# A new order of the work, and new engines for some of it, in an mLSTM and ELU feed-forward kernel

## The chip, the cores and the metric

The kernel runs on one core of a Trainium2 chip. The metric is the time of one execution on the device in microseconds (us). The core has five engines that run side by side: TensorE (PE in the rows; PEld is its loading of weights), VectorE (DVE), ScalarE (ACT), GpSimd (POOL) and SyncE (SP), which issues the transfers here. They wait for one another by semaphores. Transfers of data go over queue q1. Queue q8 moves instructions.

## What is computed

A recurrent attention (an mLSTM) over 768 steps, for 4 batches of 8 heads of size 40, and then a feed-forward layer with ELU on the 3072 rows of 320 that it gives:

```python
for t in range(S):
    m_new  = np.maximum(f_gate[:, :, t] + m, i_gate[:, :, t])
    f_stab = np.exp(f_gate[:, :, t] + m - m_new)
    i_stab = np.exp(i_gate[:, :, t] - m_new)
    C = f_stab * C + i_stab * np.einsum('bhd,bhe->bhde', vt, kt)
    n = f_stab * n + i_stab * kt
    h_tilde = np.einsum('bhde,bhe->bhd', C, qt)
    denom = np.maximum(np.abs(nq), 1.0)          # nq = n . qt
    y[:, :, t] = sigmoid(o_gate) * h_tilde / denom
h = x @ w_in                                     # 3072x320 by 320x2048
g = np.where(h > 0.0, h, np.exp(np.minimum(h, 0.0)) - 1.0)
out = g @ w_out                                  # 2048x320
```

## The kernel before

The 768 steps are cut into 6 chunks of 128. A chunk of a batch is a **tile**: 24 tiles, tile n being chunk n // 4 of batch n % 4. For each tile the kernel does the following.

- It loads q and k (line 671, into one of three buffers qk_148 to qk_150), v with k once more (677) and the output gate (682) as `vko`, and from chunk 1 on the decays `bb` (705) and `w` (695). Buffers are few, so a load waits until the last reader of its buffer is done.
- **Products** (752): 16 small matmuls of k with q for all heads. VectorE multiplies them with the decays (813).
- **Visit** (`outputs`): 32 matmuls of the state C with `bb` (833), 64 of the decayed products with v (841), and for all chunks but the last 32 of k with v for the new state (851). PE runs through all these in 1.7 us or so. VectorE or GpSimd shrinks C (868) and VectorE adds to it (879).
- **Output of the tile** (`xf`, `den`): ScalarE takes the absolute value of the denominator (886), VectorE bounds and inverts it (890, 891) and gates the output (899), VectorE or GpSimd multiplies (903), a small copy follows (342), and PE turns the result (917).

The feed-forward layer takes tiles in blocks of two or three (256 or 384 columns). For each of 16 slices of 128 of the hidden size there is a first layer of 8 matmuls (970), since each operand is split into a high and a low part, and an ELU: ScalarE (978, 981), VectorE (983), the high part `gh` by ScalarE (986), the low part `gl` by VectorE or GpSimd (988). The second layer has three matmuls for each tile (997): gh, gh, gl. Sums go to DRAM (1024) where a block is done in two goes. The weights are split on the chip as well, by conversions of many elementwise steps (lines 437 to 477), early in the kernel.

What sets the order: every operation is an `Op` with the engines that can do it and their costs. `Plan.run` is a greedy scheduler, which puts at each moment the ready operation of lowest **rank** on its engine. The rank follows from the tile or slice an operation belongs to, unless the table `PLACES` holds a number for its place (p13 for the products of tile 13 and what follows them, v13 for its visit, y13 for the output, qk13, vk13, o13, w13, bb13 for loads, c and d for conversions). The table `USES` names an engine for single operations ("p13.1" is the second operation at place p13; f is the feed-forward layer):

```python
    def at(self, place, rank):
        self.place = place
        self.rank = self.places.get(place, rank)
...
        use = self.uses.get(f"{self.place}.{nth}")
        if use is not None:
            o.engines = {use: engines[use]}
...
                    (o for o in pending if when[o] <= t), key=lambda o: (o.rank, -o.tail, o.number)
```

Where the plan leaves PE idle before 70 us, filler matmuls of ones (526) are put in. The code that comes out has no loops: each of the matmuls is an instruction of its own in the program.

Of the kernel before, what the change touches and what calls it, by code (L numbers as in the profile page):

```python
# [206 lines left out]
def tile_mlstm_then_elu_ffn(  # L207
# [48 lines left out]
    PLACES = {"clear": 7.1154181, "g0": -0.805181392, "qk0": -0.351178529, "v0":  # L256
# [22 lines left out]
    USES = {"clear.2": "POOL", "rows.0": "DVE", "rows.1": "DVE", "rows.2": "DVE",  # L279
        "states.0": "ACT", "states.2": "ACT", "g0.0": "ACT", "g0.7": "DVE", "p0.4": "ACT",  # L280
        "p0.8": "DVE", "y0.6": "DVE", "y0.8": "DVE", "p1.4": "ACT", "p1.10": "POOL", "v1.1":
        "ACT", "y1.6": "ACT", "p2.10": "POOL", "v2.1": "ACT", "p3.4": "ACT", "v3.1": "ACT",
# [4 lines left out]
        "ACT", "g2.2": "DVE", "g2.4": "POOL", "g2.10": "DVE", "p8.3": "ACT", "p8.9": "ACT",  # L287
# [19 lines left out]
        "ACT", "d3.0": "ACT", "d3.1": "DVE", "c4.0": "ACT", "c5.2": "POOL", "c6.1": "ACT",  # L307
# [5 lines left out]
        "ACT", "c17.0": "ACT", "c17.5": "DVE", "d17.0": "DVE", "f.5": "DVE", "f.12": "DVE",  # L313
# [821 lines left out]
```

## Time and profile before

| | |
|---|---|
| time, median of 3 runs | 470.45 us (469.73 to 471.0) |
| the profiled execution | 468.6 us |
| its span | 466.8 us |
| around the span | 1.8 us |
| PE busy | 98% |
| DVE, ACT, POOL busy | 72%, 60%, 22% |

The span goes from the first instruction to the last. A wait of an engine is idle time ahead of one of its instructions. The profile puts it down to the engine whose semaphore came last; where it finds none, it writes "issue".

### The profile page before, as it was taken

Reading aid. Unit: us, or ns where it says so; the run is one execution under the profiler, and the core shown is the slowest. Engines: PE = TensorE matmul, PEld = TensorE weight load, DVE = VectorE, ACT = ScalarE, POOL = GpSimd, SP = SyncE. Lnnn points to the kernel's source line nnn. Section 1 sums busy time; section 2 is a strip of 40 time slices with the busy share of each in tenths; the row PEclk is TensorE's granted clock in tenths of the full one; section 3 lists DMA queues with packets and bytes.
Section 4 is the critical chain, followed back from the end, with each engine's and each line's share of the span. In section 5 each row is a group of like instructions: output and inputs, shape, how many; then the busy total and the mean of one; then the engine's idle time right before and its main releaser. Section 6 shows DMA issues by size and latency. Waiting matters only on the chain.

```text
span 466.8 us, 13897 instructions
## 1 busy us (share of the span) xinstructions
PE 458.5 (98%) x5737; PEld 429.1 (92%) x5737; DVE 336.5 (72%) x698; ACT 277.9 (60%) x672; POOL 100.6 (22%) x137
## 2 busy tenths in 40 slices
PE   9899999999999999999999999999999999999996
PEld 4557799999999999989999999999999999999996
DVE  7899899899888878778887853587894754354432
ACT  5778678788866456454654565354545455545664
POOL 1226302320212031234111340131041201010011
PEclk9999999999999999999999999999999999999999
DMA  7956374334208361246405501353411301000100
GB/s 210 317 183 198 102 276 146 114 98 148 86 8 236 103 226 41 79 131 199 144 17 150 173 1 43 114 165 119 133 45 38 95 0 44 1 3 0 44 1 28
DMA packets 42175, 49.71 MB, mean 106 GB/s; under 512 B 3360, under 2 KB 34816, under 8 KB 42112
## 3 DMA queue, kind: packets, MB, share of 16 engines
q1 hardware_dynamic: 42112, 48.82, 33.6%
q8 instruction: 45, 0.74, 0.6%
q14 instruction: 18, 0.15, 0.1%
HBM read 43.42 MB, written 5.39 MB: 105 GB/s over the span
## 4 chain that ended last, share of the span: by engine, by line
PE 96%; DVE 2%; ACT 1%; issue 1%; DVEq 0%; ACTq 0%
PE h L970 39%; PE acc L997 36%; PE ps_a L752 6%; PE ps_a L841 3%; PE ps_a L833 3%; PE acc L526 3%; PE ps_a L917 2%; PE ps_a L851 1%; PE h L779 1%; PE h L485 1%; PE h L789 1%; PE h L783 1%; DVE gl L988 0%; DVE w L477 0%; DVE w L813 0%
## 5 line engine op out<-in xcount | busy, mean ns | idle before, releaser
L970 PE MATMUL h<-xh,w 128*128 128x384 f32 (+1 forms) x720 | 176.6, 321 | 0.0
L997 PE MATMUL acc<-w,gh 128*128 128x320 f32 x768 | 172.2, 311 | 0.9 <-ACT den L886 0.7
L997 PEld LDWEIGHTS acc<-w,gh 128*128 128x128 f32 x768 | 128.9, 188 | 2.6 <-issue 0.6
L983 DVE SCALAR_TENSOR_TENSOR e<-e,h 128x384 f32<-128x384 f32 (+1 forms) x144 | 72.7, 505 | 80.6 <-ACT e L981 79.9
L970 PEld LDWEIGHTS h<-xh,w 128*128 128x128 f32 x720 | 124.6, 188 | 1.7
L978 ACT ACTIVATE e<-h 128x384 f32<-128x384 f32 (+1 forms) x144 | 65.4, 454 | 93.3 <-PE h L970 85.4
L997 PE MATMUL acc<-w,gl 128*128 128x320 f32 x384 | 118.7, 309 | 0.5 <-DVE gl L988 0.5
L970 PE MATMUL h<-xl,w 128*128 128x384 f32 (+1 forms) x432 | 111.4, 317 | 0.0
L986 ACT CAST gh<-e 128x384 fp32r<-128x384 f32 (+1 forms) x144 | 68.1, 474 | 39.6 <-DVE e L983 38.5
L970 PEld LDWEIGHTS h<-xl,w 128*128 128x128 f32 x432 | 76.3, 188 | 0.0
L988 DVE TENSOR_TENSOR gl<-e,gh 128x384 fp32r<-128x384 f32 (+1 forms) x109 | 60.6, 558 | 20.0 <-ACT gh L986 19.7
L997 PEld LDWEIGHTS acc<-w,gl 128*128 128x128 f32 x384 | 72.0, 188 | 0.9 <-DVE gl L988 0.9
L981 ACT ACTIVATE e<-e 128x384 f32<-128x384 f32 (+1 forms) x144 | 70.5, 490 | 3.6
L988 POOL TENSOR_TENSOR gl<-e,gh 128x384 fp32r<-128x384 f32 (+1 forms) x35 | 33.5, 956 | 171.2 <-ACT gh L986 125.7
L796 DVE TENSOR_TENSOR_SCAN w<-w,ident 128x512 f32<-128x512 f32 x32 | 39.4, 1241 | 1.5 <-DMA w<-f_d 1.5
L813 DVE TENSOR_TENSOR w<-ps_a,w 128x512 f32<-128x512 f32 x48 | 31.4, 683 | 2.0 <-ACT wl L342 1.0
L752 PE MATMUL ps_a<-qk 40*128 40x128 f32 x384 | 29.9, 291 | 0.3 <-DVE xl L342 0.2
L752 PEld LDWEIGHTS ps_a<-qk 40*128 40x128 f32 x384 | 25.1, 193 | 5.2 <-issue 1.8
L903 POOL TENSOR_TENSOR xf<-xf,den 128x320 f32<-128x320 f32 x13 | 10.8, 831 | 45.0 <-DVE den L891 44.6
L841 PE MATMUL ps_a<-vko,w 128*32 128x41 f32 x1536 | 19.4, 201 | 1.0 <-DVE w L813 0.9
L841 PEld LDWEIGHTS ps_a<-vko,w 128*32 128x32 f32 x1536 | 17.7, 109 | 2.2 <-DVE w L813 1.5
L868 POOL TENSOR_TENSOR C<-C,dec 40x164 f32<-40x164 f32 x20 | 10.0, 498 | 33.2 <-PE ps_a L833 27.2
(114 smaller groups left out, 432.2 us busy)
## 6 DMA issues: line engine op xcount, KB each, us to landing
w<-f_d SPq DMA_DIRECT2D x32, 256.0 KB
vko<-in_vko SPq DMA_DIRECT2D x24, 324.0 KB
qk<-in_qk SPq DMA_DIRECT2D x48, 160.0 KB
wide<-in_w_out SPq DMA_DIRECT2D x8, 640.0 KB
wide<-in_w_in SPq DMA_DIRECT2D x8, 512.0 KB
vko<-in_vko SPq DMA_DIRECT2D x24, 160.0 KB
out<-os SPq DMA_DIRECT2D x24, 160.0 KB
bb<-b_d SPq DMA_DIRECT2D x40, 80.0 KB
```

The source lines that it names most:

```text
L526: nc.tensor.matmul(spare, ones, ones.unsqueeze(1).to_broadcast([P, 4, P]), start=True, stop=True, skip_group_check=True,)
L752: nc.tensor.matmul(ps(two, P, HH, L)[:, j, :], kt[rows, j, :], qt[rows, j, :], start=True, stop=True,)
L796: nc.vector.tensor_tensor_scan(a, a, ident4.rearrange("p h t -> p (h t)"), 0.0, op0=ALU.mult, op1=ALU.add)
L813: lambda e, half=half: nc.vector.tensor_mul(w(half), ps(half, P, HH, L), w(half)),
L841: nc.tensor.matmul(y[r, h, :], w()[:, i, r], va()[:, h, :], start=not opened, stop=(i == H - 1), skip_group_check=True,)
L970: nc.tensor.matmul(h(), a[g][:, fs], m, start=(i == 0), stop=(i == len(prods) - 1))
L978: op(act(N), lambda e, h=h, ff=ff: nc.scalar.activation(ff("e"), h(), AF.Relu, scale=-1.0), (KHP,), (KE,))
L981: lambda e, ff=ff: nc.scalar.activation(ff("e"), ff("e"), AF.Exp, scale=-1.0), (), (KE,))
L983: lambda e, h=h, ff=ff: nc.vector.scalar_tensor_tensor(out=ff("e"), in0=ff("e"), scalar=-1.0, in1=h(), op0=ALU.add, op1=ALU.max),
L986: op(act(N), lambda e, ff=ff: nc.scalar.copy(ff("gh", F32R), ff("e")), (KE,), (KG,))
L988: lambda e, ff=ff: eng[e].tensor_sub(ff("gl", F32R), ff("e"), ff("gh", F32R).bitcast(F32)),
L997: nc.tensor.matmul(acc(a), x[:, sl], bw[g][:, j, :], start=(f == f0 and i == 0), stop=(f == f1 - 1 and i == 2),)
```

## The change

Only the two tables are new: of 105 entries of `PLACES` two stay as they were and 122 stand in the new table; of 284 entries of `USES` 169 stay and 310 stand there. No operation is added to the computation or taken from it, and its functions are the same; the lines behind the tables move down by nine (752 becomes 761, 997 becomes 1006).

```diff
-    PLACES = {"clear": 7.1154181, "g0": -0.805181392, "qk0": -0.351178529, "v0":
+    PLACES = {"rows": 7.1461, "states": 7.08096, "y0": -1.19333215, "qk1": 0.293438602,
...
```

What the tables do is seen in the order of the instructions. In the names below w_118 is a part of the second layer's weights, w_113 and w_114 are parts of the first layer's, C_146 is the state of batch 2, and "x2" stands for two in a row.

PE just ahead of tile 10's visit, at about 193 to 195 us of the trace of before. Before:

```order
L970 MATMUL h<-xh,w_114 128x256
L970 MATMUL h<-xl,w_114 128x256 x2
L970 MATMUL h<-xh,w_114 128x256 x3
L752 MATMUL ps_a<-qk_149 128x128 x8
L997 MATMUL acc<-w_118,gh 128x320 x2
L997 MATMUL acc<-w_118,gl 128x320
L997 MATMUL acc<-w_118,gh 128x320 x2
L997 MATMUL acc<-w_118,gl 128x320
L970 MATMUL h<-xh,w_114 128x256
```

After:

```order
L979 MATMUL h<-xh,w_114 128x256
L979 MATMUL h<-xl,w_114 128x256 x2
L979 MATMUL h<-xh,w_114 128x256 x3
L1006 MATMUL acc<-w_118,gh 128x320 x2
L1006 MATMUL acc<-w_118,gl 128x320
L1006 MATMUL acc<-w_118,gh 128x320 x2
L1006 MATMUL acc<-w_118,gl 128x320
L761 MATMUL ps_a<-qk_149 128x128 x8
L979 MATMUL h<-xh,w_114 128x256
```

The products of tile 13 moved from ahead of the six second-layer matmuls to behind them. The visit follows in both after one more first layer (8 matmuls) and one more group of six. The loads that overwrite qk_149 wait for these products.

VectorE after the output of tile 6, at about 72 to 77 us. Before:

```order
L890 TENSOR_SCALAR den<-den 128x8
L891 RECIPROCAL den<-den 128x8
L983 SCALAR_TENSOR_TENSOR e<-e,h 128x384
L868 TENSOR_TENSOR C_146<-C_146,dec 40x4x41 x2
L342 COPY os<-acc 128x320
L988 TENSOR_TENSOR gl<-e,gh 128x384
L879 TENSOR_TENSOR C_146<-C_146,ps_a 40x4x41 x2
```

After:

```order
L899 TENSOR_SCALAR den<-den 128x8
L900 RECIPROCAL den<-den 128x8
L992 SCALAR_TENSOR_TENSOR e<-e,h 128x384
L877 TENSOR_TENSOR C_146<-C_146,dec 40x4x41 x2
L997 TENSOR_TENSOR gl<-e,gh 128x384
L351 COPY os<-acc 128x320
L888 TENSOR_TENSOR C_146<-C_146,ps_a 40x4x41 x2
```

The low part gl moved ahead of the output's copy (L997 of after is the line 988 of before). On GpSimd, beside it, a copy of `dec`, which ScalarE did before, and a narrowing now stand ahead of the multiplication of `bb` with q. On ScalarE a narrowing moved ahead of gh, and the second exponential behind it.

VectorE in the startup, at about 16 to 21 us. Before:

```order
L899 SCALAR_TENSOR_TENSOR xf<-vko,ps_a 128x320
L466 ISA narrow<-wide,narrow 128x1024
L890 TENSOR_SCALAR den<-den 128x8
L891 RECIPROCAL den<-den 128x8
L342 CAST w_114<-narrow 64x512
L903 TENSOR_TENSOR xf<-xf,den 128x320
L477 TENSOR_TENSOR w_114<-narrow,w_114 64x512
L342 COPY xf<-xf 128x64
L477 TENSOR_TENSOR w_113<-narrow,w_113 64x512
L813 TENSOR_TENSOR w<-ps_a,w 128x512 x2
```

After:

```order
L908 SCALAR_TENSOR_TENSOR xf<-vko,ps_a 128x320
L899 TENSOR_SCALAR den<-den 128x8
L900 RECIPROCAL den<-den 128x8
L475 ISA narrow<-wide,narrow 128x1024
L912 TENSOR_TENSOR xf<-xf,den 128x320
L351 COPY xf<-xf 128x64
L351 CAST w_114<-narrow 64x512
L486 TENSOR_TENSOR w_113<-narrow,w_113 64x512
L486 TENSOR_TENSOR w_114<-narrow,w_114 64x512
L822 TENSOR_TENSOR w<-ps_a,w 128x512 x2
```

The operations on `den` and `xf` moved ahead of the steps of the conversion, and all stand ahead of the multiplication of `w` as before.

Elsewhere the order is the same up to small exchanges until about 262 us. From there to about 430 us it is another one: visits stand earlier or later by some microseconds, the gates of chunk 5 much earlier, and some more of the work on `gl` and of the copies is on GpSimd (125 rows of instructions instead of 111). The last 25 us are the same. One filler matmul fewer is put in, at about 17.4 us.

## Rows read from the trace of the kernel before

**Rows 1.** The page's head: engine, busy us, share, instructions.

```profile
span 466.8 us, 13897 instructions
...
PE 458.5 (98%) x5737; PEld 429.1 (92%) x5737; DVE 336.5 (72%) x698; ACT 277.9 (60%) x672; POOL 100.6 (22%) x137
```

**Rows 2.** Waits of PE: us in total, times, longest.

```profile
PE ps_a L841 <- DVE w L813: 0.9, 1, 0.9
PE acc L997 <- ACT den L886: 0.7, 1, 0.7
PE ps_a L851 <- issue: 0.7, 1, 0.7
PE acc L997 <- DVE gl L988: 0.5, 1, 0.5
```

**Rows 3.** The page's queues: packets, MB, share of 16 engines.

```profile
q8 instruction: 45, 0.74, 0.6%
```

**Rows 4.** Timeline 193 to 200: start, us, engine, line, operation [idle before].

```profile
193.02 1.16 PE L752 MATMUL ps_a<-qk 40*128 40x128 f32 x16
...
194.12 0.56 PE L997 MATMUL acc<-w,gh 128*128 128x320 f32 x2
194.26 0.73 SPq L671 DMA_DIRECT2D qk<-in_qk  x2
...
195.10 0.28 PE L970 MATMUL h<-xh,w 128*128 128x256 f32 x1
...
197.01 0.78 PE L833 MATMUL ps_a<-C,bb 104*32 104x82 f32 x32
...
199.41 0.45 PE L997 MATMUL acc<-w,gh 128*128 128x320 f32 x2 [0.70 <-ACT den L886]
```

**Rows 5.** Windows: stretch, length, busy (count) of PE, PEld, DVE, ACT, POOL.

```profile
46.54:199.41 152.87, 151.48 (x1777) 145.90 (x1778) 131.64 (x269) 103.76 (x245) 32.31 (x46) 1.00 0.40 127
```

**Rows 6.** DMA queues in 195.1 to 195.2: packets, MB, share.

```profile
q1 hardware_dynamic: 2, 0.01, 27.4%
```

**Rows 7.** DMA queues in 195.8 to 196.8, all there is.

```profile
q1 hardware_dynamic: 66, 0.21, 56.4%
```

**Rows 8.** DMA queues in 196.8 to 197.0, the instructions' queue.

```profile
q8 instruction: 1, 0.02, 34.3%
```

**Rows 9.** DMA queues in 407.2 to 407.3, all there is.

```profile
q8 instruction: 1, 0.02, 61.4%
```

**Rows 10.** Timeline of PE, 407.6 to 410.6.

```profile
408.46 0.78 PE L833 MATMUL ps_a<-C,bb 104*32 104x82 f32 x32
```

**Rows 11.** DMA queues in 42.9 to 44.2, all there is.

```profile
q1 hardware_dynamic: 81, 0.39, 96.1%
```

**Rows 12.** Timeline 73 to 77: VectorE, ScalarE, GpSimd and PE around gl.

```profile
73.03 0.81 DVE L868 TENSOR_TENSOR C<-C,dec 40x164 f32<-40x164 f32 x2
...
73.76 0.50 ACT L986 CAST gh<-e 128x384 fp32r<-128x384 f32 x1
...
74.90 1.30 POOL L770 TENSOR_TENSOR bb<-bb,qk 104x512 f32<-104x512 f32 x1 [1.60 <-ACT dec L342]
...
75.08 1.53 DVE L988 TENSOR_TENSOR gl<-e,gh 128x384 fp32r<-128x384 f32 x1
...
76.67 0.41 PE L997 MATMUL acc<-w,gl 128*128 128x320 f32 x1 [0.47 <-DVE gl L988]
```

**Rows 13.** Timeline 16 to 26: the den operation twice, and GpSimd.

```profile
17.22 0.75 POOL L817 TENSOR_TENSOR vko<-vko,wl 128x320 f32<-128x320 f32 x1 [1.54 <-DMA vko<-in_vko]
17.31 0.69 DVE L890 TENSOR_SCALAR den<-den 128x8 f32<-128x8 f32 x1
...
25.79 0.15 DVE L890 TENSOR_SCALAR den<-den 128x8 f32<-128x8 f32 x1
```

**Rows 14.** DMA queues in 200.6 to 203.6, all there is.

```profile
q1 hardware_dynamic: 954, 0.81, 84.6%
```

**Rows 15.** DMA queues in 203.6 to 203.7, the instructions' queue.

```profile
q8 instruction: 1, 0.02, 59.5%
```

More of the change, by code (lines that the diff above doesn't have):

```diff
@@ L255, in tile_mlstm_then_elu_ffn @@
     )
-    PLACES = {"clear": 7.1154181, "g0": -0.805181392, "qk0": -0.351178529, "v0":
[22 rows of a table removed]
[L279 to L282, printed above, removed]
[4 rows of a table removed]
-        "ACT", "g2.2": "DVE", "g2.4": "POOL", "g2.10": "DVE", "p8.3": "ACT", "p8.9": "ACT",
[19 rows of a table removed]
-        "ACT", "d3.0": "ACT", "d3.1": "DVE", "c4.0": "ACT", "c5.2": "POOL", "c6.1": "ACT",
[5 rows of a table removed]
-        "ACT", "c17.0": "ACT", "c17.5": "DVE", "d17.0": "DVE", "f.5": "DVE", "f.12": "DVE",
[20 rows of a table removed]
-        "DVE", "f.1018": "POOL", "f.1039": "POOL", "f.1053": "DVE", "f.1060": "POOL",
-        "f.1067": "POOL"}
+    PLACES = {"rows": 7.1461, "states": 7.08096, "y0": -1.19333215, "qk1": 0.293438602,
[26 rows of a table added]
+    USES = {"clear.0": "POOL", "rows.0": "DVE", "rows.1": "DVE", "states.2": "ACT",
[3 rows of a table added]
+        "POOL", "y2.4": "ACT", "p3.4": "ACT", "p3.8": "ACT", "p3.10": "POOL", "v3.1": "ACT",
[27 rows of a table added]
+        "ACT", "d2.1": "DVE", "d2.2": "DVE", "d2.3": "DVE", "c3.1": "ACT", "d4.0": "ACT",
+        "c5.0": "ACT", "c5.2": "POOL", "d5.2": "ACT", "c6.0": "DVE", "d6.0": "ACT", "d6.2":
+        "ACT", "c7.1": "ACT", "c8.1": "ACT", "c8.2": "DVE", "d8.0": "ACT", "d8.1": "DVE",
[6 rows of a table added]
+        "DVE", "f.26": "DVE", "f.56": "DVE", "f.79": "DVE", "f.100": "POOL", "f.116": "ACT",
[19 rows of a table added]
+        "POOL", "f.1067": "POOL", "f.1074": "DVE"}
     plan = Plan(room, ("qk", "bb", "e", "gh", "gl", "os"))
```

151 rows, old and new, of tables (PLACES, USES) are left out of this document.

## The prediction

> **What bounds the kernel now.** I read the head of the page first [rows 1]. TensorE (PE) is busy 98% of the span; VectorE (72%), ScalarE (60%) and GpSimd (22%) have room on the whole. The change leaves the amount of matrix work as it is, apart from one filler matmul, so it can only give back moments in which PE stands still, or add some. The waits of PE come next [rows 2]: four are 0.5 us or longer, 2.8 us together (0.9 + 0.7 + 0.7 + 0.5). Apart from a wait before the first matmul, that is about the whole stock: a new order can win some 0.6%, while what it can lose has no such bound. The profiled execution took 468.6 us, 1.85 us less than the median 470.45 of the runs shown. I make the sum against 468.6 and add 1.85 at the end.
>
> **Two of these waits have a releaser that cannot be right.** The pattern to look for: the engine named has long been done, or "issue" is named. What is missing there may be the instructions themselves. Queue q8 brings 45 blocks, 0.74 MB, so 16 KB each [rows 3]. The kernel has 5737 matmuls and 5737 weight loads [rows 1]; 11474 / 45 is 255 for each block. I therefore suppose pages of 256 PE instructions. The two stalls fit: the one at 199.41 [rows 4], and the one put down to "issue" [rows 2], at 46.54. Between them PE runs 1777 matmuls and 1778 weight loads [rows 5]: 3555, against 14 pages, 3584. The missing 29, under 1%, I take for waiting instructions of PE, which the profile does not count. So both stalls sit at the same place in a page: PE comes to the end of what it has, and the next block is not there.
>
> **Why the block is late at 199.41.** The products of tile 13 end at 194.18 (193.02 + 1.16), and the loads that overwrite the buffer they have read issue at 194.26 [rows 4]. Their first packets move between 195.1 and 195.2, 0.9 us later [rows 6]. From 195.8 to 196.8 the loads fill 56% of the DMA time, and no block of q8 moves [rows 7]; it moves only in 196.8 to 197.0 [rows 8]. PE passes a page boundary at 197.01, with the first matmul of tile 10's visit [rows 4], so the block starts at most 0.2 us before it. I compare a later visit that a boundary opens in the same way, with nothing else on the queues: the block starts in 407.2 to 407.3 [rows 9], the matmul at 408.46 [rows 10], so the block is 1.2 us ahead. The loads cost the block some 1.0 to 1.1 us, and PE stood for 0.70 of it. From the block's start (196.9) to PE's next matmul (199.41) it is 2.5 us; I use that below.
>
> **The change part by part.** Only two tables change; what they do is read from the order of instructions.
>
> (a) The products of tile 13 go behind one group of six second-layer matmuls, which took from 194.12 to 195.10, 0.98 us [rows 4]. The products' end, the issue of the loads behind them and the first packets all move by that: the packets from 195.15 to 196.1. With nothing ahead of it the block starts at 197.01 - 1.2 = 195.8, some 0.3 us before the packets. It is then in place by 195.8 + 2.5 = 198.3, and the wait goes: **-0.70**. If the loads are ahead again, the block is later by their shift: **+0.9** or so. I take -0.70, because the margin, though thin, has the right sign; both ends stay for the range. Moving the products costs nothing itself: what VectorE makes of them is wanted only at tile 13's own visit, three visits on.
>
> (b) The stall at 46.54. The page there holds the same small matmuls, moved by one. In the 1.3 us before its block, a load (w_out) fills 96.1% of the DMA time [rows 11], so the block may hang on that load; on SP the load keeps its place behind the fetch of tile 6's q and k. I take **0**; if the load comes sooner, up to -0.69, if later, as much to the other side.
>
> (c) The wait for gl at 76.67 [rows 12]. gl needs gh, which ScalarE has ready at 74.26 (73.76 + 0.50). VectorE shrinks C until 73.84, copies an output, and begins gl only at 75.08; gl then took 1.53 us, while a 1.30 us multiplication of GpSimd ran beside it from 74.90. PE asked for it 0.47 us too early, at 76.20. In the new order gl stands directly behind the shrinking of C, ahead of the output's copy. gh stays where it was within some 0.2 us: on ScalarE a narrowing takes the place of the second exponential ahead of it, which now comes behind. GpSimd has a copy and a narrowing ahead of its multiplication. So gl begins by 74.5, and even at 1.53 us it ends by 76.0, before PE asks: **-0.47**. If GpSimd holds it longer, 0.
>
> (d) Startup. VectorE's short den operation took 0.69 us at 17.31, where the same one takes 0.15 us at 25.79; a GpSimd multiplication ran beside the first from 17.22 to 17.97 [rows 13]. Later PE waits 0.9 us for VectorE's w [rows 2]. Now den and its reciprocal stand before the conversion's custom operation, not behind it. If the collision goes, 0.54 us of the wait goes. If the custom operation takes the collision over, nothing does, or the wait grows by as much. The operations before the wait are the same ones, so I take the middle: **0**, with ends of -0.5 and +0.5. The filler matmul that is taken out lay in a wait of PE for ScalarE: 0.
>
> (e) From about 262 to 430 us the order is rebuilt: visits lie up to 7 us earlier or 6 us later, the gates of the last chunk some 50 us earlier. None of the four waits is there, PE has work all the time, and the changes between small and large matmuls are equal in number to within four: **0**, with the slower rival's price above it.
>
> Sum: -0.70 - 0.47 = -1.17. 468.6 - 1.17 = 467.4 for a profiled execution, and with 1.85 **469.3 us** for a median (-0.25%).
>
> **The rivals.**
>
> *Transfers do not hold the block back.* The block came late because PE asked late, the 0.70 stays whatever is queued, and only (c) is left: 470.45 - 0.47 = 470.0. For it: the pages that stalled are short in time, and in a short page any block is late. Against it: rows 7 to 10, and the block after the stall. From 200.6 to 203.6 loads fill 84.6% of the DMA time with no block of q8 among them [rows 14]; the block comes in 203.6 to 203.7, when they are done [rows 15], 4.2 us behind its boundary at 199.41. The Trainium skill, "DMA: Bandwidth & Descriptors", section "Queues, rings and completion order", speaks for this rival: each DMA engine goes round its queues packet by packet, so that a block would wait for some packets and not for a whole load. By that rule (a) is worth nothing and the sum is -0.47; rows 14 and 15 show the block waiting 4.2 us and do not agree with it.
>
> *The change of (a) misses.* The loads still lead: +0.9 - 0.47 gives 470.9.
>
> *Faster.* The startup's collision goes (-0.5): 468.8. The load of (b) comes sooner too (-0.69): 468.1.
>
> *Slower: the loads of tile 16 win.* In (e) the visit of tile 16 is followed by the loads for its freed buffers, bb, w, vko and og. In the new order a page of small matmuls follows: eight second-layer and eight first-layer matmuls, the turn and most of tile 17's visit. At 0.16 us for a large one (0.98 / 6) and 1.7 us for a whole visit (197.01 to 199.41 less 0.70 [rows 4]) it lasts some 4.3 us. If its block waits for these loads as the one in rows 14 and 15 did, it starts 4.2 us behind the boundary and serves 2.5 us later: 6.7 against 4.3, a stall of up to 2.4. That alone makes 469.3 + 2.4 = 471.7; with (a) lost too, 473.3. It decides whether the first packets of these loads come before the block's request. For it: the order is new there, and the trace of before shows none of its pages. Against it: in the old order no block of this stretch cost a listed wait, though the same loads are moved there.
>
> **How the numbers follow.** About 0.3%, 1.4 us, is what a measurement can tell from no change, so "faster" begins below 469.04 and "slower" above 471.86. Chances: forecast (468.8 to 469.7) 0.35; faster (467.4 to 468.8) 0.25; transfers do not matter 0.15 and (a) missed 0.10 (together 469.7 to 471.0); slower, at 471.7 or more, 0.15. Of the forecast's 0.35 a third, 0.12, lies below 469.04, and of the slower case one or two hundredths below 471.86. So faster 0.37, same 0.50 (0.23 + 0.25 + 0.02), slower 0.13. The range leaves out most of the slower case and the best edge of the faster one. Low is 468.1 less 0.7, what the lowest of the runs shown lies under their median: 467.4. High is 471.6, the slower rival's lower end.
>
> **What would show it.** (a): tile 10's visit runs into the next second-layer matmuls without idle time, and the block starts 1.2 us before the visit's first matmul. (b): again 0.7 us of "issue" inside the small matmuls near 46 us. (c): no wait for gl near 76. (d): the wait for w near 22 us at 0.9, or below 0.5. The prediction is wrong if the block of (a) is late again, or if a wait above 0.5 us that names an engine long done stands in 262 to 430 us, above all behind tile 16's visit.

## The result, and the profile after

The changed kernel took 474.05 us (median of 20 runs, 469.83 to 476.36), the one before 470.71 beside it (469.3 to 474.18). The ratio is 1.0054 with an interval of [1.0032, 1.0077]: slower, where I had forecast 469.3 and no higher than 471.6. Measured once more beside other runs it was 473.11 against 472.06, 1.0013 [0.9986, 1.0040], which is not clear of noise; how far executions differ is told below.

The profiled execution took 476.08 us, its span is 474.3 us, 7.5 longer than the old one [rows 1]. The page's head and the instructions' queue:

```profile
span 474.3 us, 13914 instructions
...
PE 459.5 (97%) x5736; PEld 429.5 (91%) x5736; DVE 333.8 (70%) x689; ACT 278.5 (59%) x669; POOL 108.2 (23%) x149
...
q8 instruction: 45, 0.74, 0.6%
...
PE 83%; DVE 6%; DMA 6%; issue 3%; ACT 1%; POOL 1%; SPq 0%; DVEq 0%; ACTq 0%; POOLq 0%
```

PE is busy for 1.0 us more than before, the rest is waiting. The last row is the chain that ended last: "issue", time in which the engine waited for nothing that the profile shows, is 3% of it and was 1% before, though the number of blocks is the same. The waits of PE (us in total, times, longest):

```profile
PE ps_a L860 <- issue: 4.9, 3, 2.7
PE h L788 <- ACT w L813: 1.5, 2, 0.8
PE ps_a L761 <- DMA qk<-in_qk: 1.2, 2, 0.7
...
PE h L979 <- DVE e L992: 0.9, 1, 0.9
PE acc L1006 <- issue: 0.5, 1, 0.5
```

Against [rows 2]: the wait for gl is gone, the missing blocks cost 5.4 us in four places instead of 1.4 in two. Where they lie, from PE's timeline (start, us, engine, line, operation [idle before]):

```profile
46.95 0.49 PE L860 MATMUL ps_a<-vko 128*8 128x41 f32 x29 [0.93 <-issue]
...
199.61 0.30 PE L1006 MATMUL acc<-w,gh 128*128 128x320 f32 x1 [0.47 <-issue]
...
219.73 0.27 PE L860 MATMUL ps_a<-vko 128*8 128x41 f32 x5 [1.28 <-issue]
...
306.07 0.41 PE L860 MATMUL ps_a<-vko 128*32 128x41 f32 x20 [2.69 <-issue]
```

The two stalls of before, at 46.54 and 199.41, divide both spans. Up to the first, 46.54 us became 46.95 (+0.4). From there to the second, 152.87 became 152.66 (-0.2). From the second to the end, 267.4 became 274.7 (+7.3). The loss is thus in the last part, and 6.8 of it can be read off: 1.28 at 219.73, 2.69 at 306.07, 0.93 at 344.90 (the wait for e), a wait of 0.22 at 339.99, and 1.70 that shows only in the windows behind 306 (length, busy and count of PE, PEld, DVE, ACT, POOL, then granted clock, DMA share, GB/s):

```profile
304.00:305.00 1.00, 0.00 (x0) 0.00 (x0) 0.00 (x0) 0.00 (x0) 0.00 (x0) 1.00 0.39 105
...
306.00:307.00 1.00, 0.93 (x22) 0.88 (x23) 0.26 (x1) 0.47 (x2) 0.00 (x0) 0.77 0.60 179
307.00:308.00 1.00, 1.00 (x5) 1.00 (x4) 0.97 (x4) 0.30 (x3) 0.75 (x1) 0.50 0.28 85
308.00:309.00 1.00, 1.00 (x4) 1.00 (x4) 0.97 (x3) 0.00 (x0) 0.66 (x2) 0.50 0.79 141
309.00:310.00 1.00, 1.00 (x5) 1.00 (x5) 0.12 (x1) 0.69 (x2) 0.94 (x2) 0.53 0.86 291
```

Behind the stop PE counts as wholly busy, with four or five matmuls in a microsecond: the granted clock is 0.50, which is 1.2 GHz of 2.4. What is missing from 1 in these rows, 0.23 + 0.50 + 0.50 + 0.47, is the 1.70 us. A busy share alone would have hidden it.

The stop at 306.07 stands in the visit of tile 17, at the end of the page behind tile 16's visit, where the slower rival had put it. From 295.44 on SP issues what waits for this visit's buffers, bb, w and the output gate first; the last of it (start and length of the issuing):

```profile
298.43 0.80 SPq L680 DMA_DIRECT2D qk<-in_qk  x2
299.28 0.35 SPq L686 DMA_DIRECT2D vko<-in_vko  x1
```

And the queues from 300 to 303.6 (first row) and from 303.6 to 303.7 (second row):

```profile
q1 hardware_dynamic: 872, 0.97, 91.0%
...
q8 instruction: 1, 0.02, 71.5%
```

A page of 256 PE instructions began at 298.74, when the next block should be asked for. For 3.6 us only loads move; the block starts at 303.65, 4.9 us behind the page's start, and PE, out of work at 303.38, goes on 2.4 us after that.

### The profile page after: what moved, and what is told of

Read it like the earlier page. It is cut to its first block, busy times and chain, and to the rows that moved or that the text cites. A ratio compares the mean times of both kernels' runs of the same rounds, so it can differ in the third digit from the quotient of the medians.

```text
span 474.3 us, 13914 instructions
## 1 busy us (share of the span) xinstructions
PE 459.5 (97%) x5736; PEld 429.5 (91%) x5736; DVE 333.8 (70%) x689; ACT 278.5 (59%) x669; POOL 108.2 (23%) x149
## 4 chain that ended last, share of the span: by engine, by line
PE 83%; DVE 6%; DMA 6%; issue 3%; ACT 1%; POOL 1%; SPq 0%; DVEq 0%; ACTq 0%; POOLq 0%
PE h L979 36%; PE acc L1006 35%; PE ps_a L761 4%; PE ps_a L842 3%; PE ps_a L850 2%; DMA qk<-in_qk 2%; PE ps_a L926 1%; DMA bb<-b_d 1%; DMA wide<-in_w_out 1%; DMA w<-f_d 1%; PE ps_a L860 1%; DVE w L822 1%; DVE narrow L475 1%; DVE w L486 0%; ACT wide L452 0%
## 5 line engine op out<-in xcount | busy, mean ns | idle before, releaser
L997 POOL TENSOR_TENSOR gl<-e,gh 128x384 fp32r<-128x384 f32 (+1 forms) x38 | 36.4, 958 | 185.3 <-ACT gh L995 162.7
L997 DVE TENSOR_TENSOR gl<-e,gh 128x384 fp32r<-128x384 f32 (+1 forms) x106 | 56.6, 536 | 21.9 <-ACT gh L995 20.0
L908 DVE SCALAR_TENSOR_TENSOR xf<-vko,ps_a 128x320 f32<-128x320 f32 x24 | 11.7, 486 | 11.1 <-ACT den L895 8.0
L826 POOL TENSOR_TENSOR vko<-vko,wl 128x320 f32<-128x320 f32 x12 | 10.2, 848 | 33.7 <-ACT wl L351 17.8
```

The costliest lines, as they stand in the source:

```text
L997: lambda e, ff=ff: eng[e].tensor_sub(ff("gl", F32R), ff("e"), ff("gh", F32R).bitcast(F32)),
```

## The experiments

Two helpers were added to the kernels. `MOVES` takes named operations (place and number, as in `USES`) to another place in the finished order, before any instruction is written. `HALVED = n` writes each of the first n filler matmuls as two of half the width, so that every later instruction of PE stands 2n instructions further on in its page, with the same work.

### Is it the place in the page?

The changed kernel with its pages moved by 96 instructions (e1), and the kernel before likewise (e2):

```diff
+HALVED = 48
```

> The changed kernel with 48 of its first filler matmuls cut into two halves: 48 matmuls and 48 weight loads more, no more work, so every page of 256 PE instructions ends 96 instructions earlier in the program. Theory 1 (the changed kernel lost its time to instruction blocks that came late): the waits of 1.28 us at 219.7, 2.69 us at 306.1 and 0.47 us at 199.6 go, and with the second one the 3.4 us at half the clock behind it (1.7 us): about 6.1 us less than the 476.1 us of the profiled execution, 469 to 471 us, within 0.3% of the kernel before. The wait near 46 us stays at 0.7 to 0.9. Rival (the waits are data that come late in the new order, or the new order is slower in itself): they stay where they are, and the time stays 0.5% or more above the kernel before.

Measured: 471.71 against 471.46 beside it, 1.0008 [0.9982, 1.0034], the span of the profile 469.2 us. Its waits of PE:

```profile
PE h L983 <- DVE e L996: 1.4, 2, 1.1
PE ps_a L854 <- issue: 1.3, 1, 1.3
...
PE acc L1010 <- ACT e L994: 0.9, 1, 0.9
...
PE h L983 <- issue: 0.3, 1, 0.3
```

The stops at 199.6, 219.7 and 306 are gone, and with the last of them the half clock; the loads move where they moved. Two waits of "issue" remain, 1.30 at 46.49, which is more than the 0.7 to 0.9 expected, and 0.27 at 57.12. The order of the work alone does not make the stops: it takes a page boundary ahead of a run of small matmuls. What is shown is the stops in the traces; beside the second measurement of the unaltered kernel (1.0013) the time shows no clear gain.

> The kernel before with the same 48 filler matmuls cut into halves. Theory 1: the wait of 0.70 us at 199.4 goes, since the page that ends there now ends inside other work; the wait near 46.5 stays at 0.7 to 0.9, since that page still holds two visits; 0.7 us faster, a ratio of 0.998 to 0.999. Rival (the wait at 199.4 is a late operand): it stays at 0.70, ratio 1.000.

Measured: 472.39, 1.0030 [1.0008, 1.0052]. The stop at 199.4 went as expected, but the first one grew to 1.21 (at 47.4), another of 0.52 came at 58.1, and the time is not better: this expectation was missed. A shift of all pages takes one stop away and makes another.

The two shifted kernels also show what the new order costs without these stops. From the page boundary near 231 us to the one near 435, with no stop for a block in either, the changed order took 204.3 us (e1) and the old one 202.4 (e2); 1.4 of the 1.9 are the two waits for e in the list above, at 335.52 and 339.76. So the rival of e1, that the new order is slower in itself, is right for this part.

### Do the loads hold the block back?

Behind tile 16's visit: the loads of q and k for tile 20 and of v for tile 19 were put behind a later load of the same queue (e3).

```diff
+MOVES = [(['qk20.0', 'qk20.1', 'vk19.0'], 'after', 'w20.1')]
```

> The changed kernel with three loads (q and k of tile 20, k and v of tile 19, 0.64 MB) moved on SP's queue from behind tile 16's visit to behind the decays of tile 20, which wait for tile 17's visit. The page boundaries stay where they are. Theory 1 in its form that the block queues behind the loads issued before it was asked for: 0.64 MB at 0.25 MB/us is 2.6 us, so the block that came at 303.65 comes near 301.2, the wait at 306.1 falls from 2.69 to at most 0.5 us, and the half clock behind it goes: 4 us less in the profiled execution. Rival (a page of small matmuls is too short for any block, loads or not): the wait stays at 2.2 us or more.

PE's timeline and, below it, the queues from 298 to 301.7 and from 301.7 to 301.8:

```profile
304.12 0.41 PE L869 MATMUL ps_a<-vko 128*32 128x41 f32 x20 [0.22 <-issue]
...
q1 hardware_dynamic: 1266, 0.72, 65.1%
...
q8 instruction: 1, 0.02, 58.5%
```

With less ahead of it the block comes 2.5 us behind its page's start instead of 4.9, and the stop shrinks from 2.69 to 0.22; in two more profiles of the unaltered kernel, below, it is 1.04 and 1.87. The same page, the same instructions: here the loads hold the block. A new wait of 0.80 for e came at 316.58. The time is 472.86, 1.0005 [0.9981, 1.0029], no clear gain.

At 199.4 in the kernel before: the loads of tile 13 that my step (a) had blamed were moved behind the visit (e7).

```diff
+MOVES = [(['qk13.0', 'qk13.1'], 'after', 'o13.0')]
```

> The kernel before, with the loads of tile 13's q and k moved on SP's queue from 194.3 us to behind those of v, k, the output gate and the decays, after 200 us, so that no load moves while the block for the page boundary at 197 us is fetched. Theory 1 of the prediction (the loads hold this block back by 1.0 to 1.1 us): the block starts 0.3 to 1.2 us ahead of the boundary, and the wait of 0.70 at 199.4 falls to 0.3 or less. Rival (the page is simply short and the block has its own pace): the block starts within 0.2 us of the boundary and the wait stays at 0.6 to 0.8.

From 194 to 198.3 now no packet moves on any queue. The block's queue in 198.3 to 198.5, then PE:

```profile
q8 instruction: 1, 0.02, 35.4%
...
198.54 0.78 PE L842 MATMUL ps_a<-C,bb 104*32 104x82 f32 x32
...
200.94 0.45 PE L1006 MATMUL acc<-w,gh 128*128 128x320 f32 x2 [0.70 <-ACT den L895]
```

The block starts at the boundary again and the wait is 0.70, to the hundredth what it was with the loads [rows 4]. At this place the loads hold nothing back; that fits a block that is asked for as its page begins, and not before. (One run, 469.99 us.)

The opposite of the first edit: two more transfers of 0.33 MB each behind tile 16's visit, which copy an input to a place that nothing reads (e11).

```diff
+            if o.label == "o19.0":
+                self.extra()
```

> The changed kernel with two more transfers of 0.33 MB each, to a place in DRAM that nobody reads, among the loads behind tile 16's visit. Theory 1 (the block queues behind the loads that were issued before it was asked for): the block that came 3.4 to 4.9 us behind its boundary comes 5 to 7.5 us behind it, and PE waits 3 to 5 us there, with half the clock behind it. Rival (the loads only happen to be there): the wait stays between 1.0 and 2.7 us.

The first two rows are SP's, the next three the queues in 300 to 302.9, in 302.9 to 303.1 and in 303.1 to 305, the last is PE's:

```profile
298.20 1.20 SPq L1109 DMA_DIRECT2D nowhere<-in_vko  x2
...
300.13 0.77 SPq L683 DMA_DIRECT2D qk<-in_qk  x2
...
q1 hardware_dynamic: 654, 0.93, 95.9%
...
q8 instruction: 1, 0.02, 29.6%
...
q1 hardware_dynamic: 394, 0.54, 97.0%
...
305.40 0.41 PE L863 MATMUL ps_a<-vko 128*32 128x41 f32 x20 [1.32 <-issue]
```

A stop of 3 to 5 us was expected; 1.32 came (473.53 us, one run). The extra issues took SP's time, so the loads of q and k were issued at 300.13 and not at 298.43. The page began at 299.4, between the extra transfers and these loads; the block went in at 302.9, in the midst of full traffic that went on behind it. That fits a block that waits for transfers queued before it was asked for and passes those queued after; total traffic is not what counts. It is an inference, since no row shows when a block is asked for, and it fits only roughly: in the first profile, 101 of the 128 packets of the load issued at 299.28, 0.5 us behind the page's start, moved ahead of the block as well.

### What a stop does to the clock

In the kernel before, three of the operations on gl were put on GpSimd and done 3, 4 and 7 times, late, where hardly a load moves (e5).

```diff
+AGAIN = {"f.851": 3, "f.907": 4, "f.976": 7}
```

> The kernel before, with the low part gl of three steps late in the kernel computed 3, 4 and 7 times over on GpSimd (0.96, 0.96 and 0.74 us each), so that PE has to wait for it: by the times of one, stops of about 1.1 us near 385 us, 2.4 us near 409 and 4.0 us near 440, with nothing wrong about instructions. It measures by itself what a stop costs beyond its own length. Theory 1: the stop of 2.69 us in the changed kernel was followed by 3.4 us at half the clock because PE stood still, whatever for; then the clock here stays whole behind the first stop and falls to half for 3 to 4 us behind the second and the third, 1.5 to 2 us each. Rival (the clock fell for a reason of its own near 306 us): it stays whole behind all three.

The first stop was 1.32 at 394.74. The second and the third, and the windows behind them (columns as above):

```profile
419.08 0.41 PE L1000 MATMUL acc<-w,gl 128*128 128x320 f32 x1 [2.63 <-POOL gl L991]
...
450.82 0.41 PE L1000 MATMUL acc<-w,gl 128*128 128x320 f32 x1 [4.40 <-POOL gl L991]
...
421.00:423.00 2.00, 2.00 (x81) 1.75 (x82) 0.56 (x1) 1.06 (x3) 0.00 (x0) 1.00 0.00 0
...
452.00:454.00 2.00, 2.00 (x10) 2.00 (x10) 0.74 (x2) 0.79 (x3) 0.00 (x0) 0.50 0.01 4
```

The clock stayed whole behind 1.32 and 2.63 and fell to 0.50 behind 4.40. So a stop alone, without loads and without a missing block, brings the half clock. But 2.63 did not here and 2.69 did in the changed kernel: the length of the stop is not the whole condition, and what else counts was not found.

### How far one execution differs from another

The changed kernel again, unaltered, twice (e6 and e12):

> The changed kernel once more, unaltered, beside the others on one chip, with a second profile. Theory 1: the wait behind tile 16's visit (2.69 us at 306.1) is there again, at 1.5 us or more, with the half clock behind it, since the loads lead by several microseconds; the wait of 1.28 us at 219.7 may be there or not, since its block came 1.5 us sooner with the loads moved elsewhere. Time again 0.3 to 0.9% above the kernel before. Rival (the profiled execution was an unlucky one): the wait at 306 is gone, and the time is within 0.3%.

> The changed kernel once more, unaltered, on the chip of the last three, for how far the wait behind tile 16's visit differs from execution to execution: 1.0 to 2.7 us by the two profiles so far. If it is below 0.3, the loads do not always lead.

The stop behind tile 16's visit was 1.04 in one (473.11 us, the ratio given at the top) and 1.87 in the other (473.52), with a whole clock behind both; the 1.28 at 219.73 was in neither.

The block started 3.4 us behind the page's start in the one, 4.1 in the other, 4.9 in the first profile. The mechanism is there in all three, its size varies.

The kernel before, unaltered, once more (e16):

> The kernel before, unaltered, a second profile. If its waits differ from execution to execution by the startup's loads, as in the other runs, there are waits of 0.3 to 0.9 us before 16 us that the first profile did not have, perhaps with half the clock behind them, and its three waits at 46.5 (0.7 to 1.3), 76.7 (0.47) and 199.4 (0.7 to 1.0) are there again; 470 to 473 us. The rival: the startup is the same in all executions.

472.91 us. The old stops stood again near 50, 80 and 203 (0.65, 0.48 and 0.72), all later, because the startup went otherwise; one of 0.29 came at 222.43, at the page end where the changed kernel once had 1.28:

```profile
12.99 0.38 PE L779 MATMUL h<-mask,ident_b 128*128 128x512 bf16 x1 [2.63 <-ACT w L804]
...
16.00:18.00 2.00, 2.00 (x18) 1.77 (x22) 1.93 (x5) 1.44 (x3) 0.50 (x1) 0.50 1.00 331
```

The first profile of before had no such stop. The first 20 us are thus no property of either order: between executions of the same code they differ by more than anything my step (d) was about. In 12 of the 18 traces, of both orders, a stretch at a granted clock of 0.50 lies in the first 20 us; in e6 it follows stops of only 0.71 and 0.66.

### Are the two small gains real?

In the kernel before, only the two moves that steps (a) and (c) rested on, gl ahead of the output's copy and the products behind the six matmuls (e4):

```diff
+MOVES = [(['f.65'], 'before', 'f.58'), (['p10.0'], 'after', 'f.410')]
```

> The kernel before with two moves alone: the low part gl ahead of the output's copy on VectorE (near 75 us), and tile 10's products behind one group of six second-layer matmuls on PE (near 194 us). By the sum of the prediction both waits go: 0.47 at 76.7 and 0.70 at 199.4, 1.2 us, ratio 0.9975. By what the changed kernel's trace shows at the same two places: no wait for gl, but 0.47 us left of the other, so 0.7 us, ratio 0.9985. Rival (the moves do not set these waits): both stay.

The wait for gl went: gl took 0.56 us, since GpSimd's multiplication began only behind it, at 75.19. The stretch between the two stalls shrank by 0.46 (152.41 against 152.87), although the wait at its end did not go: 0.98 instead of 0.70. 471.41 us, 1.0011 [0.9982, 1.0040].

From here on the second move is another one: a group of 8 first-layer matmuls (f.14) goes ahead of the visit of tile 5, which puts large matmuls into the page of small ones that ended in the stall at 46.54. With it and gl (e15), with 24 instructions of shift alone (e14), and with all of it (e13):

```diff
+MOVES = [(['f.65'], 'before', 'f.58'), (['f.14'], 'before', 'v5.0')]
+HALVED = 12
```

> The kernel before with the two moves alone: no fillers more, page boundaries where they were. Theory: the waits near 46.5 and 76.7 go, 0.7 + 0.47 us; the wait at 199.4 stays at 0.7, since its boundary has not moved. 1.2 us, a ratio of 0.996 to 0.999. Rival: the wait near 46.5 only moves to the next page's end.

> The kernel before with only the page boundaries moved by 24 instructions (12 of the first fillers cut into halves). Theory: the wait of 0.70 at 199.4 goes, since the boundary now falls into the large matmuls ahead of tile 10's visit and the next page holds more of them; the waits near 46.5 (0.7 to 1.3, its page still holds two visits) and near 76.7 (0.47, gl) stay. 0.7 us, a ratio of 0.996 to 0.999. Rival: the wait at 199.4 belongs to the visit and moves with it.

> The kernel before with the two moves of the ninth run (gl near 75 us, one first-layer group between the visits near 44 us), without its 12 extra fillers, and with 12 of the first fillers cut into halves instead, so that the page boundaries stand 24 instructions earlier, as they did there. Theory (what counts is where the page boundaries fall): the waits at 46.5, 76.7 and 199.4 are all gone, as in the ninth run, and its 2.2 us of fillers too: 2 us below the ninth run, a ratio of 0.988 to 0.993. Rival (the fillers themselves did it, or the ninth run's sample was lucky): 0.994 to 1.000.

Against 472.28 beside them: the moves alone 469.99, 0.9967 [0.9937, 0.9997]; the shift alone 471.16, 0.9983 [0.9954, 1.0013], since it takes the stop at 199.4 away and the first one is 1.79, at 49.8; both together 468.04 (seven runs), **0.9925 [0.9895, 0.9955]**, faster than either kernel of this study. Its waits of PE, apart from the one before the first matmul:

```profile
PE ps_a L769 <- DMA qk<-in_qk: 1.6, 3, 0.7
...
PE ps_a L858 <- DVE w L830: 0.9, 1, 0.9
PE ps_a L868 <- issue: 0.3, 1, 0.3
```

One stop for a block is left, 0.3, and none for gl. Against the first profile of before the stops are 1.55 us less (0.69 + 0.47 + 0.70 - 0.31); the other half of the 3.5 us that the ratio stands for is not read off. The seven runs lie within 2.2 us, and what became of the longer executions of the kernel before is open. An earlier form of the same (e9; the moves put other numbers of fillers in, 12 more) had 470.30 against 471.75:

> The kernel before with two moves: gl ahead of the output's copy near 75 us, as in the fourth experiment, and one first-layer group of 8 large matmuls moved from behind tile 5's visit to between the visits of tiles 3 and 5 (near 44 us), so that the page of instructions that ends at 46.5 lasts some 0.8 us longer. Theory (a wait of this kind is a page that PE runs through before the next block is there, so a page with more large matmuls in it has none): the wait of 0.7 to 0.9 us at 46 to 48 us falls to 0.2 or less, the wait for gl is gone; from the second page boundary behind the startup on, 0.5 us less than before, and 0.7 us less ahead of it: 1.2 us in all, a ratio of 0.997 to 0.999, within what a measurement can tell from no change. Rival: the wait is a transfer that holds the block until 44.3, and it only moves behind the next matmuls.

0.9949 [0.9920, 0.9977], with all three stops gone and some 2.2 us of fillers too many.

### What stays in the changed kernel

The loads of e3, and on VectorE work for tile 22 moved behind steps of the feed-forward layer (e8):

```diff
+MOVES = [(['qk20.0', 'qk20.1', 'vk19.0'], 'after', 'w20.1'),
+         (['p22.7', 'p22.3', 'p22.4'], 'after', 'f.740')]
```

> The changed kernel with the three loads behind tile 16's visit later, as in the third experiment, and on VectorE the second scan of tile 22's decays and its multiplication of bb with q behind five steps of the feed-forward layer. Theory: the scan waited 1.1 us for its load while the steps that PE needed stood behind it on VectorE; so the wait of 0.74 to 0.93 us near 342 to 345 goes as well as the one at 306, and the profiled execution is 0.7 us or more below that of the third experiment outside the startup; a ratio of 0.997 to 1.000 to the kernel before. Rival: the wait near 342 stays, because what is late is another operation.

The second move concerns VectorE in the changed kernel, where a scan for tile 22 waits for its load:

```profile
338.26 1.22 DVE L805 TENSOR_TENSOR_SCAN w<-w,ident 128x512 f32<-128x512 f32 x1 [1.11 <-DMA w<-f_d]
...
344.29 1.02 DVE L992 SCALAR_TENSOR_TENSOR e<-e,h 128x384 f32<-128x384 f32 x2
```

The work behind it on VectorE is late by 1.11, and PE waits 0.93 for e at 344.90. With both moves the stops at 306 and 344 are 0 and 0.27 (one of 0.57 came at 314.7), and the time is 471.57, 1.0009 [0.9982, 1.0037]. To this, two exponentials on ScalarE were moved ahead of a step of a conversion (e10):

```diff
+         (['f.50', 'f.51'], 'before', 'c8.0'),
```

> The changed kernel with the loads behind tile 16's visit and the scan of tile 22 moved as in the eighth experiment, and on ScalarE the two exponential steps of the feed-forward layer near 67 us moved ahead of the conversion's absolute value, which waits there for its weights' load. Theory: the wait of 0.25 to 0.94 us near 69 us, which came with the changed kernel, is that load through ScalarE's queue; it goes, and the stretch from the page boundary near 47 to the one near 200 us falls from 152.6 to 153.2 us to 152.4 or less, as in the kernel before with gl moved alone. Rival: it stays, because something else on ScalarE is late.

472.67, 1.0016 [0.9990, 1.0041]: missed, the wait that had been near 69 stood at 72.98 with 1.05, and now for w instead of e. VectorE's rows there:

```profile
71.61 0.49 DVE L469 TENSOR_SCALAR narrow<-narrow 128x640 f32<-128x640 f32 x1 [1.41 <-ACT narrow L455]
72.02 0.82 DVE L495 TENSOR_TENSOR w<-narrow,w 128x640 fp32r<-128x640 f32 x1
```

With the exponentials ahead of it the absolute value on ScalarE comes later (at 70.80); a narrowing of VectorE waits for it, and the w that PE wants stands behind that on VectorE. The new order only exchanged one wait for another. A wait there is 0.25 to 1.05 in five of the eight traces of the changed kernel and its variants, and in none of the kernel before and its variants. In the four of them where PE waits for e (the first, e1, e6 and e8) ScalarE had waited 0.34 to 1.06 for a load of w_out ahead of the absolute value, and in no trace of the kernel before. The time at which this load is issued does not settle it: counted from the first stop it is 12.2 us in e8, which has the wait, and 13.3 in e3, which does not. Why it lands late in some executions only is open.

## Why the prediction was wrong, step by step

**Pages of 256 instructions, stalls at their ends: right.** 45 blocks as before, every "issue" at a boundary, and moving the pages moved the stalls (e1, e2). With PE's semaphore instructions, which the trace records and the busy counts leave out, there are 3584 instructions between the two stalls of before, 14 times 256 exactly: the 29 that I took for waiting instructions are these. The first stall of each profile lies between 46.5 and 50.5 us.

**(a) -0.70: wrong.** Three things failed. First, "the block is 1.2 us ahead" when nothing is queued rested on one row of before [rows 9, 10]. Two other pages of before begin within the first matmuls of a visit, with hardly a load around, by the count of instructions at 157.39 and 314.86. Their blocks, in 156.8 to 156.9 and in 314.5 to 314.6:

```profile
q8 instruction: 1, 0.02, 66.1%
...
q8 instruction: 1, 0.02, 65.4%
```

They are 0.5 and 0.3 us ahead, and the 1.2 was the exception. Second, the loads were not the cause: without them (e7) the wait is 0.70 still. In the changed kernel and its variants it is 0.39 to 0.70 where the pages were not moved, and 0.98 where the products alone were moved (e4). What sets it is the short page: PE runs through it in 1.7 us, and no block served PE sooner than 2.2 us after it started to move. Third, I misread whose products these are. They are tile 10's own (p10), the loads behind them are tile 13's; VectorE's work on them is wanted by the visit that follows at once, not "three visits on". That cost nothing in the trace, the visit began at 197.10 against 197.01, but it was luck. The rival *transfers do not hold the block back* was right at this place.

**(b) 0: right.** 0.93 against 0.69 at the same page, 0.84 and 0.97 in the changed kernel's other two profiles: up to 0.3 more, inside the ends that I gave.

**(c) -0.47: right alone, given back here.** Alone (e4) the move gave -0.46. In the changed kernel PE does not wait for gl, yet not for my reason: gl still took 1.54 us beside GpSimd, three times the 0.53 it takes elsewhere (0.56 at this place in e4), and ended at 76.48; PE was itself later and asked for it then:

```profile
74.70 1.37 POOL L779 TENSOR_TENSOR bb<-bb,qk 104x512 f32<-104x512 f32 x1
...
74.94 1.54 DVE L997 TENSOR_TENSOR gl<-e,gh 128x384 fp32r<-128x384 f32 x1
...
76.68 0.31 PE L1006 MATMUL acc<-w,gl 128*128 128x320 f32 x1
```

"By 74.5" was missed by 0.4, and a new wait near 69 took back 0.25 of the gain in this profile and 0.9 in another; the other 0.2 is not read off.

**(d) 0: the size of the ends was wrong.** The startup differs between executions of one code by waits of 0.3 to 2.6 us and often by a stretch at half clock (e16). What I had named as the sign did change: the wait of 0.9 for w near 22 us stands in no trace of the changed order, but in seven of its eight PE waits 0.6 to 0.8 for ScalarE shortly before instead (0.80 at 20.02 in the first). What part the den operations or the filler have in that is not shown.

**(e) 0: this is the step that failed; it cost 1.8 to 5.7 us, and the slower rival was the case.** The rival was written down with its place, its page of small matmuls and its price; what I mis-sized was its chance, 0.15. Its terms against the first profile: block 4.2 us behind the boundary, measured 4.9; PE on again 2.5 later, measured 2.4; a page of 4.3, measured 4.6 (298.74 to 303.38). "Up to 2.4" was 2.69, 1.87 and 1.04 in three profiles. My argument against it, that the same loads cost nothing in the old order, was empty, since their place against the pages had changed. Two costs were not in it at all: the half clock (1.70, once in three), and waits for data that the new order brings with it (0.7 to 1.1 us near 340 to 345). From the boundary near 237 us to the one near 438 the same program took 201.2 before (201.1 to 201.5 in four more traces of the old order, e4, e7, e15 and e16), and 206.9, 204.3 and 203.0 in the three profiles after, 201.6 where the causes found were undone (e10). The stops and waits read off account for nearly all of it: 2.69 + 1.70 + 0.93 + 0.22 of 5.7, 1.87 + 1.10 of 3.0, 1.04 + 0.71 of 1.8.

So the sum should have been: (c) given back, (a) -0.1 to -0.3, and (e) +1.8 to +5.7 by the three profiles. The medians give +3.3 (474.05 - 470.71) and +1.1 (473.11 - 472.06); that the smaller one comes from smaller stops is likely but not shown.

The slower rival and *transfers do not hold the block back* both hung on the question whether loads hold a block back, and I let rows from 200.6 to 203.6 [rows 14, 15] decide it for both places. They were right for 306 (e3, e11) and wrong for 199.4 (e7), because there the block starts with its page, loads or not. The Trainium skill, "DMA: Bandwidth & Descriptors", section "Queues, rings and completion order", lets each DMA engine go round its queues packet by packet. The 3.6 us in which 0.97 MB passed ahead of one block do not look like that, the block of e11 that went in amid full traffic does; since no row shows when a block is asked for, the rule is neither shown nor refuted here, and the "do not agree" of my prediction was too strong. The Trainium skill, "Runtime: NRT & Kernel Launch", section "Instruction fetch mechanics", calls the cost of a block's boundary mostly hidden; stops of 0.2 to 2.7 us at boundaries with small matmuls behind them show where it is not.

## What to carry to other kernels

Where a kernel is written out without loops, count instructions from a known stall in steps of a block, mark the blocks that consist of small matmuls, and look at what is queued for transfer when each begins: these places, not the averages, decide what a new order costs. A stop whose releaser is "issue" or a long finished engine is moved by shifting the instructions (here 24 of them, with one group of matmuls and one step of VectorE moved: 0.75% faster, of which the stops explain about half), and each shift has to be looked at along the whole program, since it makes new stops. Before resting a term on one row, look for the other places of the same kind in the same trace, and before resting it on one profile, take a second.

## What the runs showed of the hardware that I had not expected

- Behind tile 16's visit a block of instructions with loads queued ahead of it started 3.4 to 4.9 us after its page's start; with the queues empty one moved at once (e7). PE went on 2.2 to 2.8 us after the start of its block at every stop for one, so that a page of 1.7 us has a stop even without loads (0.70 in e7).
- A stop can cost more than its length: behind 2.69 us (in the changed kernel), 2.63 (in the startup, e16) and 4.40 (e5) PE worked on at half clock, for 1.7 us of loss in the first. Behind 1.32, 1.87 and another 2.63 it did not; in the startup it did behind 0.71 and 0.66 (e6).
- The same program's stops for blocks differ from one execution to the next by up to 1.65 us at one place (1.04 to 2.69), as much as 0.35% of the time.
